# A new order of four queues in the middle of a one-core convolution and MLP kernel

## The chip, the cores and the metric

The kernel runs on one core of a Trainium2 chip. A core has five engines with an instruction queue each: TensorE (PE, matmuls, with PEld for its weight loads), VectorE (DVE), ScalarE (ACT), GpSimd (POOL) and SyncE (SP, which here only issues DMAs). Each queue runs in order; between queues there are semaphores. The metric is device time in microseconds (us) of one execution.

## The reference: what is computed

The inputs are x = A_q, k and v, each 2048 x 448 in bf16, filters for k, and the weights of an MLP that works along the 2048 positions. Cut to what matters:

```python
def _layernorm(x, axis=-1, eps=1e-5):
    ...
    return (x - m) / jnp.sqrt(v + eps)

    def _A_ref(q, k, v, shift_k, ssm_k, ssm_D):
        ...
        for t in range(ks):
            k_shift = k_shift + k_pad[:, t:t + S, :] * shift_k[:, ks - 1 - t][None, None, :]
        kv = k_shift * v
        ...
        y_f = kv_f * kf_f[None, :, :, :]
        ...
        y = y + kv * ssm_D[None, None, :]
        return q * y

    def _B_ref(x, w1, b1, w2, b2):
        h = _layernorm(x, axis=-1)
        u = jnp.einsum("bsd,sf->bdf", h, w1) + b1
        u = _gelu(u)
        y = jnp.einsum("bdf,fs->bds", u, w2) + b2
        ...

    x = A_q
    h = x + _A_ref(_layernorm(x, axis=-1), A_k, A_v, A_shift_k, A_ssm_k, A_ssm_D)
    h2 = h + _B_ref(_layernorm(h, axis=-1), B_w1, B_b1, B_w2, B_b2)
    return h2
```

kv_f and kf_f are the transforms of kv and of ssm_k, padded to twice the length: a causal convolution over 2048 positions.

## The kernel before

Positions are split as 128 partitions x 16 rows (position = 16 x partition + row). The convolution is a real transform made of matmuls in stages with a shuffle across partitions between them. In the order of the data:

- kv: transposes and small matmuls that apply the shift filter, multiplied by v (L1026).
- Stage 1 of the transform, "k1" for the filter and "u1" for kv (L1078): 16 steps each of 8 matmuls into a pair of PSUM banks. One evacuation copies the pair (128 x 896) to SBUF (op 8, L1088, or L1086 where ssm_D is added). Behind every second step three DMAs shuffle what two evacuations left (ops 9 and 10 on POOL, op 11 on SP, L1094): k1.3:9 is op 9 of step k1.3 and carries steps 2 and 3 of that block.
- Stage 2, "k2" and "u2" (L1113): 16 steps each of 4 matmuls into a pair of banks. Steps come in twos; the odd one carries the two evacuations (ops 4 and 5; L740 on ACT and L743 on DVE for k2, which scale; L739 and L742 for u2). An evacuation needs the matmuls of both steps, as it overwrites what they read.
- Products and the inverse's first stage, "i1": 16 products on DVE (L1180, 128 x 1792, op 0 of a step; a ring of four buffers), and eight groups of 16 matmuls (L1197) with two evacuations each (ops 9 and 18, or 8 and 17; L739, L742). Four DMAs behind a group shuffle its result (L1221; L1208 for the last group, i1.16). The first product waits for all shuffles of stage 1.
- The inverse's second stage "i2", one row after the other (L1323, L1329), with the gate q = layernorm(x): rows 0 to 3 are normalised beforehand ("xn", L1290 on ACT, L1292 on DVE); of the others the gate multiplies by 1/std first (L1339 on ACT, L1341 on DVE). Then a combination with x (L1349, L1359), and the statistics of the result: its sum from DVE, its squares from ACT (L1377), and a chain of five small instructions on POOL for two rows at a time (L1387, L1390, L1392, L1397 and L1401, a power of -1/2), behind which DVE writes the normalised row (L1408).
- The MLP: "mlp.r" for r = 0 to 15 are 7 matmuls of row r with the first half of w1 (L1455), accumulating over all rows into seven banks; mlp.17 to mlp.23 are those with the second half (L1465), gelu on ACT (L1445), then the second product (L1477) with the last addition on DVE (L1480).
- Beside it: "q" are the statistics of x, step q.(g+1) for rows 2g and 2g+1 (bn_stats L1257 as ops 0 and 2, aggregates L1259 as ops 1 and 3; ops 4 and 5 on POOL add epsilon, L1265, and take the power, L1268; for rows 4 to 15 they stand in every second step and serve four rows). "ct" are transposes of the table E into ET (L1127; ct0 the first eight, ct.0 to ct.2 the others), each group with one 16-bit copy of 128 x 1024 (L739 or L742). "ew" prepares a table on POOL, "warm" are two spare matmuls.

The order of the instructions isn't found by a compiler here. The program builds a list of operations, and the table ORDER gives each engine's queue word for word as step:op (a range where ops follow each other). An operation that two engines can do runs on the one whose table names it. A second table, SLOTS, names the PSUM bank (0 to 7) that each group of matmuls gets. Waits follow from that: an instruction waits for what it reads, and the first matmul of a group for the evacuation of the group that had its bank before.

```python
            self.eng[W].wait_ge(self.csem[E], n)
...
        FX = ("act", "dve")
...
                    for q_, a, nu in (("pool", 0, 8), ("pool", 96, 8), ("sp", 32, 16)):
...
                    aft = [x for w in wbufs for x in w.readers] if i == 0 else [mfirst[0]]
```

The first of these lines makes the waits of one engine for another, the second says which engines may evacuate, the third are the three shuffles behind stage 1, and the last is what the products wait for.

Of the kernel before, what the change touches and what calls it, by code (L numbers as in the profile page):

```python
# [30 lines left out]
        "mlp.19:4 mlp.7:0 mlp.19:5 mlp.8:0 mlp.19:6 mlp.7:4 mlp.9:0 mlp.9:2 mlp.8:6 mlp.9:6 mlp.8:1 mlp.9:5 mlp.9:1 "
        "mlp.8:4 mlp.10:2 mlp.10:1 mlp.10:6 mlp.9:4 mlp.19:7 mlp.10:0 mlp.10:5 mlp.10:4 mlp.10:3 mlp.11:0 mlp.11:5 "
        "mlp.11:3-4 mlp.11:1-2 mlp.11:6 mlp.12:0-6 mlp.13:0-6 mlp.14:6 mlp.14:4 mlp.14:1 mlp.14:5 mlp.14:3 mlp.15:6 "
        "mlp.15:5 mlp.15:4 mlp.15:1 mlp.19:8-15 mlp.14:0 mlp.21:0-15 mlp.17:0-8 mlp.14:2 mlp.20:0-7 mlp.22:0-7 "
        "mlp.17:9-15 mlp.20:8-15 mlp.18:0-15 mlp.15:2 mlp.23:0-7 mlp.15:0 mlp.22:8-15 mlp.15:3 mlp.23:8-15 "
        "mlp.24:0-13 mlp.25:0-13 mlp.26:0-13 mlp.27:0-13 mlp.28:0-13 mlp.29:0-13 mlp.30:0-13 mlp.31:0-13 mlp.32:0-13 "
        "mlp.33:0-13 mlp.34:0-13 mlp.35:0-13 mlp.36:0-13 mlp.37:0-13 mlp.38:0-13 mlp.39:0-10 mlp.39:16-17 mlp.39:11 "
        "mlp.39:18-20 mlp.39:12 mlp.39:21-22 mlp.39:13 mlp.39:23-29 "
# [4 lines left out]
        "k1.7:8 u1.6:8 tables.9:5 u1.8:8 u1.9:8 u1.10:8 k2.1:4-5 u1.12:8 u1.13:8 u1.14:8 u1.15:8 k2.9:5 k2.5:5 "  # L43
        "ct0.0:8 k2.7:4 k2.3:5 u2.1:4 k2.15:4-5 u2.13:4 u2.7:4-5 k2.11:4-5 u2.9:5 i1.1:9 i1.1:18 u2.11:5 i1.14:9 "
        "i1.14:18 u2.11:4 i1.10:18 i1.8:18 u2.5:5 u2.3:5 i1.10:9 u2.3:4 i1.12:18 i1.12:9 i1.6:18 u2.15:5 u2.15:4 "
        "i1.4:17 i1.4:8 i1.16:18 i1.16:9 xn.1:0 xn.5:0 xn.2:0 xn.4:0 ct.0:8 ct.1:8 ct.2:8 i2.46:0 i2.29:0 i2.19:0 "
        "i2.55:0 i2.22:0 i2.33:0 i2.59:0 i2.31:0 i2.35:0 i2.68:0 i2.72:0 i2.44:0 i2.48:0 i2.81:0 i2.57:0 i2.61:0 "
        "i2.94:0 i2.70:0 i2.98:0 i2.74:0 i2.83:0 i2.87:0 i2.96:0 i2.100:0 mlp.16:5-6 mlp.16:1 mlp.21:16 mlp.17:16 "
# [8 lines left out]
        "u1.7:8 k1.2:8 k1.3:8 q.1:1 q.3:0 q.1:2 q.2:0 k2.13:4 q.1:3 q.2:1 k2.13:5 u1.11:8 q.2:3 q.3:2 k2.9:4 k2.5:4 "  # L57
        "q.4:2 k2.7:5 k2.3:4 u2.1:5 i1.0:0 u2.13:5 i1.1:0 i1.14:0 i1.13:0 u2.9:4 i1.8:0 q.4:3 i1.7:0 i1.10:0 i1.9:0 "
        "i1.8:9 i1.12:0 u2.5:4 i1.11:0 i1.6:0 q.3:3 q.4:0 i1.5:0 i1.3:0 xn.0:1 q.4:1 i1.2:0 i1.6:9 i1.16:0 i1.15:0 "
        "q.3:1 q.5:2 q.6:2 q.5:3 xn.3:1 q.6:0 q.7:2 q.5:0-1 q.6:1 q.6:3 q.8:0 q.8:2 q.7:0 q.7:3 i2.3:0 i2.11:0 "  # L60
        "i2.4:0 i2.12:0 i2.5:0 i2.13:0 i2.6:0 i2.14:0 i2.18:0 i2.8:0 i2.21:0 i2.30:0 i2.16:0 q.8:1 i2.42:0 i2.34:0 "
        "bias.1:0 i2.26:0 q.8:3 i2.27:0 q.7:1 i2.47:0 i2.43:0 q.8:4 i2.56:0 i2.39:0 i2.60:0 i2.40:0 i2.85:0 i2.52:0 "
        "i2.53:0 i2.73:0 i2.69:0 i2.95:0 i2.65:0 i2.66:0 i2.82:0 i2.86:0 i2.99:0 i2.78:0 i2.79:0 i2.105:0 i2.92:0 "
        "i2.91:0 i2.104:0 mlp.24:14 mlp.25:14 mlp.26:14 mlp.27:14 mlp.28:14 mlp.29:14 mlp.30:14 mlp.31:14 mlp.32:14 "
        "mlp.33:14 mlp.34:14 mlp.35:14 mlp.36:14 mlp.37:14 mlp.38:14 mlp.39:14 mlp.39:30 "
# [8 lines left out]
        "tables.9:10 u1.9:9-10 k1.3:9-10 tables.9:9 u1.13:9-10 q.1:4 u1.11:9 u1.15:10 u1.15:9 u1.11:10 tables.9:11 "  # L74
        "q.1:5 ew.0:3 ew.0:0 q.2:4 xn.0:0 ew.0:1-2 i1.1:19 i1.1:21 i1.14:19 i1.14:21 i1.8:19 i1.8:21 i1.10:19 "
        "i1.10:21 i1.12:19 i1.12:21 q.2:5 i1.6:19 i1.6:21 i1.6:20 i1.4:20 i1.16:21 q.4:4 xn.3:0 i1.16:22 q.6:4-5 "
        "q.4:5 i1.4:19 i1.4:21 i2.7:0 i2.15:0 i2.23:0-2 i2.24:0 i2.25:0 i2.36:0-2 i2.37:0 i2.38:0 q.8:5 i2.49:0-2 "
        "i2.50:0 i2.51:0 i2.62:0-2 i2.63:0 i2.64:0 i2.75:0-2 i2.76:0 i2.88:0 i2.77:0 i2.88:1 i2.101:0-1 i2.88:2 "
        "i2.101:2 i2.102:0 i2.89:0 i2.90:0 i2.103:0 i2.0:0 "
# [30 lines left out]
        "mlp.39:16:1 "  # L110
# [1429 lines left out]
```

## Time and profile before

| what | us |
|---|---|
| runs (3), median | 171.01 |
| lowest and highest run | 170.82 and 174.45 |
| the profiled execution, its own time | 170.75 |
| span of the profiled execution, first to last instruction | 168.9 |
| busy in the span: PE, DVE, ACT, POOL | 160.1, 99.8, 92.5, 60.2 |

Some 1.85 us of the profiled execution's time lie outside its span. TensorE is busy 95% of the span by the records, but a matmul record lasts longer than the time to the next matmul, so this says little of single stages; the waits and the stretches say more. In a row of a timeline stand the start in us, the time up to the end of the last instruction in it, engine, line, operation, output<-input with shapes, the count, and in brackets the idle time just before and what ended it. In a row of the stretches each engine has its busy time, with the number of its instructions in brackets.

### The profile page before, as it was taken

Reading aid. Unit: us, or ns where it says so; the run is one execution under the profiler, and the core shown is the slowest. Engines: PE = TensorE matmul, PEld = TensorE weight load, DVE = VectorE, ACT = ScalarE, POOL = GpSimd, SP = SyncE. Lnnn points to the kernel's source line nnn. Section 1 sums busy time; section 2 is a strip of 40 time slices with the busy share of each in tenths; the row PEclk is TensorE's granted clock in tenths of the full one; section 3 lists DMA queues with packets and bytes.
Section 4 is the critical chain, followed back from the end, with each engine's and each line's share of the span. In section 5 each row is a group of like instructions: output and inputs, shape, how many; then the busy total and the mean of one; then the engine's idle time right before and its main releaser. Section 6 shows DMA issues by size and latency. Waiting matters only on the chain.

```text
span 168.9 us, 3572 instructions
## 1 busy us (share of the span) xinstructions
PE 160.1 (95%) x1416; PEld 92.8 (55%) x1416; DVE 99.8 (59%) x197; ACT 92.5 (55%) x134; POOL 60.2 (36%) x157
## 2 busy tenths in 40 slices
PE   6999999888998999889999999999999999999994
PEld 2885775423323433344445555555577777777783
DVE  4978898999999999999879230000003213132231
ACT  3699868899999999999787703103550000000000
POOL 8103749997910545885887800000000000000000
PEclk9999999999999999999999999999999999999999
DMA  5999799887749456658999999930000111101111
GB/s 162 420 331 385 243 307 347 307 319 241 231 99 352 128 187 183 194 165 276 390 400 402 426 419 420 415 131 0 0 0 7 51 54 54 54 0 58 54 54 54
DMA packets 15564, 35.15 MB, mean 208 GB/s; under 512 B 3804, under 2 KB 9644, under 8 KB 15548
## 3 DMA queue, kind: packets, MB, share of 16 engines
q1 hardware_dynamic: 12396, 28.26, 45.8%
q0 software_dynamic: 3008, 6.58, 12.1%
q8 instruction: 11, 0.18, 0.4%
q10 hardware_dynamic: 144, 0.08, 0.2%
q14 instruction: 5, 0.04, 0.1%
HBM read 22.05 MB, written 1.84 MB: 141 GB/s over the span
## 4 chain that ended last, share of the span: by engine, by line
PE 67%; DVE 13%; ACT 8%; POOL 6%; issue 2%; DMA 2%; DVEq 0%; ACTq 0%; POOLq 0%
PE ps L1477 25%; PE ps L1465 13%; PE ps L1455 11%; DVE arena L1180 6%; ACT arena L740 4%; POOL arena L1094 4%; PE ps L985 3%; PE ps L1044 3%; PE ps L1057 3%; ACT arena L739 3%; PE ps L1078 2%; PE ps L1197 2%; ACT arena L1088 2%; DMA arena<-arena 2%; DVE arena L742 2%
## 5 line engine op out<-in xcount | busy, mean ns | idle before, releaser
L1480 DVE SCALAR_TENSOR_TENSOR arena<-ps,arena 128x448 bf16<-128x448 f32 (+2 forms) x17 | 11.1, 656 | 57.0 <-PE ps L1477 57.0
L1477 PE MATMUL ps<-arena 128*128 128x448 bf16 (+2 forms) x238 | 42.7, 342 | 0.0
L1477 PEld LDWEIGHTS ps<-arena 128*128 128x128 bf16 x238 | 33.3, 145 | 9.5
L1455 PE MATMUL ps<-arena 128*128 128x448 bf16 x112 | 24.8, 353 | 0.2
L1465 PE MATMUL ps<-arena 128*128 128x448 bf16 x112 | 23.3, 352 | 0.0
L739 ACT CAST arena<-ps 128x896 bf16<-128x896 f32 x26 | 21.8, 968 | 0.6 <-PE ps L1113 0.2
L1088 ACT CAST arena<-ps 128x896 bf16<-128x896 f32 x24 | 20.3, 914 | 2.1 <-PE ps L1078 1.6
L1445 ACT ACTIVATE arena<-ps,arena 128x448 bf16<-128x448 f32 x14 | 8.2, 632 | 20.4 <-PE ps L1465 10.3
L1094 POOL DMA_DIRECT2D arena<-arena x32 | 17.9, 562 | 3.5 <-ACT arena L1088 2.9
L1180 DVE TENSOR_TENSOR arena<-arena 128x1792 bf16<-128x1792 bf16 x16 | 16.8, 1083 | 0.1
L1455 PEld LDWEIGHTS ps<-arena 128*128 128x128 bf16 x112 | 10.8, 98 | 11.0 <-DVE arena L1408 1.5
L1113 PE MATMUL ps<-arena 128*64 128x448 bf16 x128 | 15.7, 361 | 1.0 <-ACT arena L739 0.5
L1465 PEld LDWEIGHTS ps<-arena 128*128 128x128 bf16 x112 | 11.0, 98 | 10.2
L1078 PE MATMUL ps<-arena 128*32 128x448 bf16 x256 | 14.8, 355 | 1.6 <-DVE arena L1026 0.5
L1197 PE MATMUL ps<-arena 64*128 64x448 bf16 x128 | 13.7, 351 | 1.1 <-DVE arena L1180 0.5
L1221 POOL DMA_DIRECT2D arena<-arena x16 | 9.5, 596 | 14.0 <-ACT arena L739 13.5
L1113 PEld LDWEIGHTS ps<-arena 128*64 128x64 f16 x128 | 5.2, 108 | 10.8 <-ACT arena L739 3.2
L1197 PEld LDWEIGHTS ps<-arena 64*128 64x128 f16 x128 | 5.1, 94 | 9.5 <-ACT arena L739 3.4
L739 ACT COPY arena<-ps 128x1024 bf16<-128x1024 bf16 (+2 forms) x10 | 9.4, 966 | 1.7 <-PE ps L985 1.5
L1026 DVE TENSOR_TENSOR arena<-ps,arena 128x512 bf16<-128x512 f32 (+1 forms) x16 | 9.4, 619 | 0.7 <-PE ps L1011 0.7
L1078 PEld LDWEIGHTS ps<-arena 128*32 128x32 f16 x256 | 5.2, 95 | 8.3 <-ACT arena L1088 1.7
L1408 DVE TENSOR_SCALAR arena<-arena 128x448 bf16<-128x448 f32 x16 | 7.7, 511 | 3.5 <-POOL arena L1401 3.5
(102 smaller groups left out, 198.3 us busy)
## 6 DMA issues: line engine op xcount, KB each, us to landing
arena<-in_B_w_dram SPq DMA_DIRECT2D x8, 896.0 KB, 10.0
arena<-in_B_w_dram SPq DMA_DIRECT2D x2, 2048.0 KB, 17.4
arena<-arena SPq DMA_DIRECT2D x16, 224.0 KB, 3.6
arena<-arena POOLq DMA_DIRECT2D x32, 112.0 KB, 3.3
arena<-in_B_w_dram SPq DMA_DIRECT2D x2, 1536.0 KB, 19.3
arena<-arena POOLq DMA_DIRECT2D x13, 196.0 KB, 3.8
arena<-in_A_k_dram SPq DMA_DIRECT2D x4, 448.0 KB, 5.5
arena<-in_A_v_dram SPq DMA_DIRECT2D x4, 448.0 KB, 8.4
```

The source lines that it names most:

```text
L739: return e.copy(out=dst(), in_=src())
L1078: op("pe", lambda e, W, b=b, r=r, q=q, x=x, c0=c0: e.matmul(PS[32 * q:32 * q + 32, b.slots[x], 0:D], E[:, 2 * r + x, c0:c0 + 32], src[:, r ...
L1088: return e.copy(out=dst, in_=Ppair(b)) if W == "act" else e.tensor_copy(out=dst, in_=Ppair(b))
L1094: shuf[tag].append(op(q_, lambda e, W, g=g, i=i, a=a, nu=nu, jh=jh: e.dma_start(T[a + i:a + i + 4 * nu - 3:4].rearrange("p (j k) c d -> p ...
L1113: op("pe", lambda e, W, b=bs[h], h=h, j=j, c=c, par=par: e.matmul(PS[64 * par:64 * par + 64, b.slots[c], 0:D], FW[:, 64 * c:64 * c + 64], ...
L1180: op("dve", lambda e, W, m=m, i=i: e.tensor_tensor(out=MR(m.slots[0]).rearrange("p (x y) d -> p x y d", x=2), in0=TU[:, i].unsqueeze(2).br ...
L1197: k = op("pe", lambda e, W, b=bs[h], m=ms[h], par=par, t=t, tab=tab, xy=xy, P=P: e.matmul(Pb(b, par), tab[P, :], MR(m.slots[0])[P, xy, :], ...
L1221: op(q_, lambda e, W, j=j, p0=p0, a=a, b_=b_, j0=j0: e.dma_start(TZ[p0:p0 + 29:4, j0:j0 + (b_ - a) // 8].rearrange("p r c d -> p r (c d)") ...
L1455: op("pe", lambda e, W, r=r, fc=fc, b=bs[fc]: e.matmul(Pb(b), W1A[:, r, 128 * fc:128 * fc + 128], Q[:, r, :], start=(r == 0), stop=(r == R ...
L1465: op("pe", lambda e, W, r=r, fc=fc, b=b: e.matmul(Pb(b), W1B[:, r, 128 * (fc - n0):128 * (fc - n0) + 128], Q[:, r, :], start=(r == 0), sto ...
L1477: op("pe", lambda e, W, r=r, fc=fc, b=b, d0=d0, d1=d1: e.matmul(Pb(b)[:, d0:d1], W2[fc // 7][:, fc % 7, r:S:R], G[:, fc, d0:d1], start=(fc ...
L1480: op("dve", lambda e, W, r=r, b=b, A=A, d0=d0, d1=d1: e.scalar_tensor_tensor(out=XR(r)[:, d0:d1], in0=Pb(b)[:, d0:d1], scalar=bm[:, r:r + ...
```

## The change

Only the two tables change. The PE, ACT, DVE and POOL rows are in another order from behind the evacuation of k1.3 (DVE), behind u1.9's first shuffle (POOL), behind k2.1 (ACT) and behind k2.0 (PE) up to the end of i2. Twelve operations go from ACT to DVE (ct0.0:8, k2.15:5, k2.3:5, k2.5:5, u1.14:8, u2.1:4, u2.3:5, u2.7:4, u2.9:5, xn.1:0 and the gates i2.59:0 and i2.81:0), eleven from DVE to ACT (k2.13:5, k2.3:4, k2.5:4, u1.11:8, u2.1:5, u2.13:5, u2.9:4, i1.6:9, i1.8:9 and the gates i2.42:0 and i2.85:0). SP's order and the number of instructions are as before, and POOL's DMAs keep their order among themselves. PSUM banks are given out anew from ct0 on. Of the diff, the head of DVE's changed part:

```diff
-        "u1.7:8 k1.2:8 k1.3:8 q.1:1 q.3:0 q.1:2 q.2:0 k2.13:4 q.1:3 q.2:1 k2.13:5 u1.11:8 q.2:3 q.3:2 k2.9:4 k2.5:4 "
+        "u1.7:8 k1.2:8 k1.3:8 q.1:1 q.2:3 q.1:2 q.3:0 q.4:2 q.1:3 q.2:0 q.3:1 q.2:1 q.4:3 ct0.0:8 k2.13:4 q.3:2 "
```

What stands in the queues, as queue rows (number, line, operation, output<-input, count, and for POOL the semaphores it waits for). First POOL from the shuffles of u1.9 and k1.3 to those of u1.11, before:

```order
68 L1094 DMA arena<-arena 8x4x1792 [waits csem_act]
69 L1094 DMA arena<-arena 8x4x1792
70 L1094 DMA arena<-arena 8x4x1792 [waits csem_dve]
71 L1094 DMA arena<-arena 8x4x1792
72 L891 TENSOR_TENSOR arena<-arena 128x128
73 L1094 DMA arena<-arena 8x4x1792 [waits csem_act]
74 L1094 DMA arena<-arena 8x4x1792
75 L1265 TENSOR_SCALAR arena<-arena 128x2 [waits csem_dve]
76 L1094 DMA arena<-arena 8x4x1792 [waits csem_dve]
77 L1094 DMA arena<-arena 8x4x1792 [waits csem_act]
78 L1094 DMA arena<-arena 8x4x1792 x2
```

And now:

```order
68 L1094 DMA arena<-arena 8x4x1792 [waits csem_act]
69 L891 TENSOR_TENSOR arena<-arena 128x128
70 L894 TENSOR_SCALAR arena<-arena 128x128 [waits csem_pool]
71 L1265 TENSOR_SCALAR arena<-arena 128x2 [waits csem_dve]
72 L1094 DMA arena<-arena 8x4x1792 x3
73 L1094 DMA arena<-arena 8x4x1792 [waits csem_act]
74 L1094 DMA arena<-arena 8x4x1792
75 L1094 DMA arena<-arena 8x4x1792 [waits csem_act]
76 L1265 TENSOR_SCALAR arena<-arena 128x2
77 L1094 DMA arena<-arena 8x4x1792 [waits csem_dve,csem_act]
78 L1094 DMA arena<-arena 8x4x1792 x2
```

The statistic q.1:4 (L1265) has moved from behind u1.13's two DMAs to a place between u1.9's first and second; rows 72 are u1.9:10 and both of k1.3. A second one, q.2:4, now stands ahead of u1.15's and u1.11's last DMAs.

DVE in the same place, from the statistics behind k1.3 to the first product (L1180), before:

```order
59 L1088 CAST arena<-ps 128x896
60 L1259 BN_AGGR arena<-arena 128x2
61 L1257 BN_STATS arena<-arena 128x6
62 L743 TENSOR_SCALAR arena<-ps 128x896 x2
63 L1257 BN_STATS arena<-arena 128x6
64 L743 TENSOR_SCALAR arena<-ps 128x896 x2
65 L742 CAST arena<-ps 128x896
66 L1180 TENSOR_TENSOR arena<-arena 128x1792
67 L742 CAST arena<-ps 128x896
68 L1180 TENSOR_TENSOR arena<-arena 128x1792 x3
```

And now:

```order
57 L1257 BN_STATS arena<-arena 128x6
58 L1259 BN_AGGR arena<-arena 128x2 x3
59 L742 COPY arena<-ps 128x1024
60 L743 TENSOR_SCALAR arena<-ps 128x896
61 L1257 BN_STATS arena<-arena 128x6
62 L743 TENSOR_SCALAR arena<-ps 128x896 x2
63 L1088 CAST arena<-ps 128x896
64 L743 TENSOR_SCALAR arena<-ps 128x896 x3
65 L742 CAST arena<-ps 128x896 x2
66 L1180 TENSOR_TENSOR arena<-arena 128x1792 x2
67 L742 CAST arena<-ps 128x896
68 L1180 TENSOR_TENSOR arena<-arena 128x1792 x7
```

The copy of ct0 (L742 COPY) has come to DVE, nine evacuations instead of eight lie ahead of the first product, and behind the second product there is one evacuation and then seven products in a row.

Last POOL's chain of the i2 statistics, from the power of rows 2 and 3 to that of rows 6 and 7, before:

```order
87 L1401 TENSOR_TENSOR arena<-arena 128x2
88 L1387 TENSOR_SCALAR arena<-arena 128x2
89 L1390 TENSOR_TENSOR arena<-arena 128x2
90 L1392 TENSOR_TENSOR arena<-arena 128x2
91 L1397 TENSOR_SCALAR arena<-arena 128x2
92 L1401 TENSOR_TENSOR arena<-arena 128x2
93 L1268 TENSOR_TENSOR arena<-arena 128x4
94 L1387 TENSOR_SCALAR arena<-arena 128x2
```

And now:

```order
86 L1401 TENSOR_TENSOR arena<-arena 128x2
87 L1221 DMA arena<-arena 8x2x896
88 L1387 TENSOR_SCALAR arena<-arena 128x2
89 L1390 TENSOR_TENSOR arena<-arena 128x2
90 L1268 TENSOR_TENSOR arena<-arena 128x4
91 L1392 TENSOR_TENSOR arena<-arena 128x2
92 L1387 TENSOR_SCALAR arena<-arena 128x2
93 L1397 TENSOR_SCALAR arena<-arena 128x2
94 L1401 TENSOR_TENSOR arena<-arena 128x2
```

A DMA of i1.4 (L1221), which stood ahead of the chain, and the power q.8:5 (L1268) now lie inside it, and sums of the next two rows (the second L1387) go ahead of a power.

106 rows, old and new, of tables (ORDER, SLOTS) are left out of this document.

## The prediction

> **What bounds the kernel now.** I read the table of stretches first, then the groups of instructions by line, the waits, and last the timelines of single engines.
>
> ```profile
> core 0: us, PE busy (x) PEld busy (x) DVE busy (x) ACT busy (x) POOL busy (x), PEclk, DMA share, GB/s
> 36.00:55.00 19.00, 17.14 (x172) 6.00 (x168) 18.97 (x27) 18.69 (x24) 9.62 (x21) 1.00 0.71 234
> 55.00:71.00 16.00, 14.83 (x141) 5.63 (x137) 15.87 (x25) 15.65 (x20) 9.64 (x16) 1.00 0.59 173
> 71.00:76.00 5.00, 4.10 (x32) 2.36 (x33) 4.78 (x13) 5.00 (x8) 4.39 (x9) 1.00 0.57 170
> 82.20:124.00 41.80, 41.80 (x222) 21.46 (x223) 12.69 (x36) 18.28 (x39) 12.24 (x30) 1.00 0.72 285
> ```
>
> From 82.2 us on TensorE has no idle time at all, and the matmuls there are the same in number before and after the change. Before that, from 36 to 71 us, it is ScalarE (18.69 of 19.00 and 15.65 of 16.00) and VectorE (18.97 and 15.87) that are full: they drain PSUM, and TensorE waits for free banks. So the change is worth what it moves the moment at which the dense matmuls begin, and nothing else. The waits say the same:
>
> ```profile
> PEld ps L1197 <- ACT arena L739: 3.4, 10, 0.6
> PEld ps L1113 <- ACT arena L739: 3.2, 7, 0.7
> PEld ps L1197 <- DVE arena L1180: 1.5, 2, 1.0
> ```
>
> The prices of one instruction come from the groups (busy time, mean ns):
>
> ```profile
> L739 ACT CAST arena<-ps 128x896 bf16<-128x896 f32 x26 | 21.8, 968 | 0.6 <-PE ps L1113 0.2 <-PE ps L1197 0.2
> L742 DVE CAST arena<-ps 128x896 bf16<-128x896 f32 x6 | 6.5, 1085 | 0.0
> L742 DVE COPY arena<-ps 128x1024 bf16<-128x1024 bf16 x9 | 5.8, 685 | 1.1 <-PE ps L1057 1.1
> L1257 DVE BATCH_NORM_STATS2 arena<-arena 128x6 f32<-128x448 bf16 x16 | 9.2, 612 | 0.0
> ```
>
> Instructions of one engine overlap a little at their ends, so what counts is start to start. On the timelines:
>
> ```profile
> 36.30 1.73 ACT L740 ACTIVATE arena<-ps 128x896 bf16<-128x896 f32 x2
> 42.86 1.01 ACT L739 COPY arena<-ps 128x1024 f16<-128x1024 f16 x1
> 43.75 1.80 ACT L740 ACTIVATE arena<-ps 128x896 bf16<-128x896 f32 x2
> 45.77 0.91 ACT L739 CAST arena<-ps 128x896 bf16<-128x896 f32 x1 [0.22 <-PE ps L1113]
> 52.37 12.40 ACT L739 CAST arena<-ps 128x896 bf16<-128x896 f32 x15
> 67.39 3.69 ACT L739 CAST arena<-ps 128x896 bf16<-128x896 f32 x4
> 33.98 2.09 DVE L1086 TENSOR_TENSOR arena<-ps,arena 128x896 bf16<-128x896 f32 x2
> 36.20 1.68 DVE L1257 BATCH_NORM_STATS2 arena<-arena 128x6 f32<-128x448 bf16 x3
> 47.03 1.08 DVE L1180 TENSOR_TENSOR arena<-arena 128x1792 bf16<-128x1792 bf16 x1
> 69.06 0.18 DVE L1259 BATCH_NORM_AGGREGATE arena<-arena 128x2 f32<-128x6 f32 x1
> 59.88 0.57 PE L1113 MATMUL ps<-arena 128*64 128x448 bf16 x4 [0.24 <-ACT arena L739]
> 60.47 0.93 PE L1197 MATMUL ps<-arena 64*128 64x448 bf16 x8
> ```
>
> With a backlog ScalarE takes an evacuation every (12.40-0.97)/14 = 0.82 us. The 1024-wide copy ct0 costs it 43.75-42.86 = 0.89. VectorE's evacuations and products follow each other at 1.085-0.085 = 1.00, its 16-bit copies at 0.60, statistics at 0.53 (three took 1.68). A group of four matmuls takes 0.57, one of eight 0.93, each about 0.1 behind the drain that frees its bank. ScalarE's last drain of this stage ends at 67.39+3.69 = 71.08; VectorE's last product ends at about 69.1, where the aggregate stands.
>
> **The change, part by part.** Counting the tables: 12 instructions go from ScalarE to VectorE (ct0, eight evacuations, xn.1, two gates i2.59 and i2.81), 11 go back (nine evacuations, gates i2.42 and i2.85). SyncE's order is unchanged.
>
> Work up to the last product: ScalarE loses eight evacuations and ct0 and gains nine, 0.82-0.89 = -0.07 us. VectorE loses nine, gains eight and ct0, 0.60-1.00 = -0.40. No row has an f16 copy on VectorE; between the bf16 copy of that size (0.60) and the f32 pace stretched to 1024 (1.00 x 1024/896 = 1.14) I take the row with 16-bit data. The page "VectorE: DVE Perf Modes" of the Trainium skill (Why PSUM operands drop a tier) lets any 16-bit PSUM copy run up to twice as fast as an f32 one; that too would be 0.60 here, where the f32 pace would leave -0.40+0.54 = +0.14. The six statistics ahead of the last product stay six, in other places: nothing.
>
> So the sums give at most a few tenths; the waits decide. I walk the new order with the spacings above, each matmul group starting 0.1 behind the drain of its banks. ScalarE: k2.1 twice from 36.30, u1.12, k2.13, u1.13, k2.5, k2.9, u1.11, u1.15, k2.15, k2.3, k2.7: the twelfth ends at 46.9, where before the twelfth ended at 45.77+0.91 = 46.68, with waits of 0.1 to 0.2 for matmuls on five of them. VectorE: the first product i1.0 starts at 48.97 instead of 47.03, with one evacuation and the copy (1.6) more behind it, so 0.3 of waits. Then u2.7 waits for its matmuls, which wait for banks that ScalarE drains (u2.13): about 0.45 idle between i1.1 and u2.7. From there VectorE has 18 more products and evacuations, one statistic and small ones: the last product ends at 69.2, against 69.1. ScalarE runs on at 0.82 and less, waits about 0.3 at i1.6, and drains i1.16 by 71.2 against 71.08. VectorE's gain of 0.40 is eaten by its two new waits. Term: +0.1.
>
> Shuffles: on POOL a statistic (q.1:4) now stands ahead of three DMAs (u1.9, and both of k1.3). It needs the aggregate of row 1, which VectorE reaches behind k1.3, two aggregates and three statistics.
>
> ```profile
> 36.18 2.18 POOL L1094 DMA_DIRECT2D arena<-arena  x4
> 39.92 1.12 POOL L1094 DMA_DIRECT2D arena<-arena  x2 [1.09 <-ACT arena L1088]
> DMA to landing us min/median/max: 3.9/4.0/4.4
> DMA to landing us min/median/max: 2.8/2.8/2.9
> DMA to landing us min/median/max: 3.3/3.4/3.7
> ```
>
> (The landing lines are those of POOL's L1094 issued from 36 to 38.5, from 39 to 41.2 and from 41.2 to 44.) Before, the four of 36.18 (u1.9, k1.3) went out without a break and the last began at 37.8. Now: k1.3's evacuation ends at 36.07, statistics run to 37.9, aggregate to 38.05, q.1:4 to 38.35, then three issues of 0.55, so k1.3's last begins at 39.45, 1.65 later. Behind it stand u1.13's issues, which wait for ScalarE until 40.4 anyway. Who needs k1.3: the groups k2.14 and k2.15, which by the walk could start at 42.95. With 3.4 to landing it is there at 42.85: no wait. With 2.8 the same; with 4.4 it lands at 43.85 and TensorE, then ScalarE and VectorE, stand 0.9. In the same way u1.11's last DMA starts at 45.1 (behind q.2:4), landing at 48.5 (up to 49.5), against the first product at 48.97: 0, up to 0.5. I take +0.1 for both together, since the middle row hides them and its margins are 0.1 and 0.5; ends 0 and +1.4. The page "DMA: Bandwidth & Descriptors" of the Trainium skill (Anatomy of one DMA) gives 2.0 us + bytes/436e3 for such a transfer; its estimate for 112 KB is 2.26 us, k1.3 landing at 41.7 and this term at 0. The trace disagrees: none of these rows is under 2.8.
>
> From the last drain to the dense matmuls:
>
> ```profile
> 71.13 1.69 PE L1323 MATMUL ps<-arena 128*128 128x448 bf16 x8 [0.26 <-ACT arena L739]
> 75.55 2.82 PE L1329 MATMUL ps<-arena 128*128 128x448 bf16 x14 [0.76 <-DMA arena<-arena]
> 78.77 0.59 POOL L1387 TENSOR_SCALAR arena<-arena 128x2 f32<-128x2 f32 x1 [0.66 <-DVE arena L1359]
> 80.47 1.07 POOL L1401 TENSOR_TENSOR arena<-arena 128x2 f32<-128x2 f32 x1
> 81.58 0.52 DVE L1408 TENSOR_SCALAR arena<-arena 128x448 bf16<-128x448 f32 x1 [0.52 <-POOL arena L1401]
> 82.14 0.68 PEld L1455 LDWEIGHTS ps<-arena 128*128 128x128 bf16 x5 [0.57 <-DVE arena L1408]
> 96.92 6.43 PE ps L1455 x34
> ```
>
> The transposes ct.1, ct.2, ct.0 now all run ahead of i2.9 and i2.1, while ScalarE still drains i1.16: cover instead of idle, but the matmuls i2.45 wait for the last transfer of i1.16 (row at 75.55), and that is issued behind ScalarE's last drain, so they start 0.1 later and the transposes gain nothing. Then i2.54, moved to fourth, waits about 0.3 for the bank of i2.45 (gate i2.46), and VectorE's statistics, 0.6 longer in front of i2.3 with xn.1 among them, make the first two normalised rows 0.6 to 1.0 late. None of it reaches the end: the third row's matmuls (mlp.2) are 32 matmuls behind i2.45 in both orders, 32 x 0.189 (6.43/34) = 6.06, and at 82.14 they waited for the chain from i2.21 over POOL (78.77, 80.47) to i2.26 (81.58). In the walk i2.21 starts at 78.03, before it started at 77.99; so this gate again moves 0.1, the same 0.1 as above.
>
> The tail of that chain:
>
> ```profile
> 95.58 1.38 POOL L1401 TENSOR_TENSOR arena<-arena 128x2 f32<-128x2 f32 x2
> 97.00 1.78 DVE L1408 TENSOR_SCALAR arena<-arena 128x448 bf16<-128x448 f32 x4 [2.18 <-POOL arena L1401]
> ```
>
> mlp.12 stands 120 matmuls behind i2.45 in both orders, at 98.83; its row came out of VectorE third of the last four, at 98.36. POOL now carries a DMA (i1.4:21, about 0.56) and i2.0 (0.2) inside this chain instead of outside, and the pow of rows 8 and 9 stands behind sums of rows 10 and 11. By the count of matmuls in front of them, rows 4, 5, 6, 8 and 9 of the MLP start 0.2 to 2.7 us later in the new order and rows 7, 10 and 11 up to 1.5 earlier; in the walk each of their rows is out of VectorE at least 0.3 before that, so only mlp.12 is tight: POOL ends its last pow between 97.0 (nothing lost) and 97.75, and mlp.12 waits 0 to 0.7. I take 0.2.
>
> Sum against the profiled execution (170.75 us; span 168.9): 170.75 + 0.1 + 0.1 + 0.2 = 171.15, forecast 171.2. The median of the runs shown, 171.01, lies 0.26 above that execution and one of the three lies 3.4 above it.
>
> **The rivals.** Faster: ScalarE's order may really close its waits. From 36.30 to 71.08 it took 34.78 us for 41 drains; at 0.82 throughout it would need 33.6, so up to 1.1 us goes, and the time is 169.65 to 170.6. For it: eight evacuations that come in pairs are now split over both engines (k2.13, k2.5, k2.9, k2.15, k2.3, u2.9, u2.1), so one pair's banks come free together. Against: VectorE is as full, and my walk gives the waits back. Slower, by one mechanism: k1.3's last shuffle lands later than 3.5 us from its issue. From there on each tenth is a tenth on both draining engines; at 4.4 it is +0.9, and 171.15-0.1+0.9 = 171.95, with u1.11's at its end 172.5. For it: the nearest window (36 to 38.5) has 3.9 to 4.4. Against: the issues are now spread out as in the window with 2.8. A third, that POOL's tail sets the end, is 171.65 at its end of +0.7, and lies in the forecast's own range.
>
> **How the numbers follow.** Forecast (170.6 to 171.8): 0.52. Faster order (down to 169.65): 0.25. Late shuffle (171.8 to 172.6): 0.15. Something not seen: 0.08. The range 169.5 to 172.7 takes both rivals in. A difference of 2%, 3.4 us, is about what a measurement of this kernel can tell from no change; no bound above reaches it, so faster and slower than that get only what is unseen: 0.03 and 0.04, within 2% 0.93.
>
> **What would show it.** Right: ScalarE's last i1 drain at 71.2 within 0.3; VectorE's first product near 49.0; q.1:4 ahead of k1.3's DMAs with their last issue near 39.5; i2.45 near 75.65; mlp.2 near 82.2; no gap on TensorE behind 82.3 but at mlp.12. Wrong: a gap of over 0.3 on TensorE before k2.14 (late shuffle), or the last i1 drain before 70.5 (faster order), or more than 0.5 us idle on TensorE behind 83 us (a chain I took as covered).

## The result, and the profile after

| | before | changed |
|---|---|---|
| median of the runs, us | 171.58 | 173.52 |
| a second series, us | 171.20 | 173.46 |
| profiled execution: own time, us | 170.75 | 173.75 |
| its span, us | 168.9 | 171.9 |

The changed kernel is slower: ratio 1.0124, 95% interval 1.0092 to 1.0155, and in the second series 1.0129 (1.0101 to 1.0158). That is about 2.1 us: less than the 2% that the prediction named as the least difference to count, but clear of noise here, as neither interval comes near 1, and 0.8 us above the range's upper end.

The profiled execution of the changed kernel is 3.0 us longer than that of before, and this splits in two. One half comes from its first 13 us, code that is the same in both kernels (TensorE's timeline with three waits that before doesn't have, and the start of k2.1; the last column in brackets is the idle time ahead and what ended it):

```profile
7.75 0.96 PE L1057 MATMUL ps<-arena 128*128 128x128 bf16 x12 [0.20 <-DMA arena<-in_A_ssm_k_dram]
9.01 0.71 PE L1057 MATMUL ps<-arena 128*128 128x128 bf16 x8 [0.30 <-DMA arena<-in_A_ssm_k_dram]
12.72 0.49 PE L1057 MATMUL ps<-arena 64*128 64x64 bf16 x5 [0.30 <-DMA arena<-in_A_ssm_k_dram]
36.80 0.95 PE L1113 MATMUL ps<-arena 128*64 128x448 bf16 x8
```

TensorE waits for loads of the filter, and k2.1 (L1113, the first matmuls of stage 2, still the same in both orders) starts at 36.80 where it started at 35.31 before. In twelve profiles of this study (the first one of each hybrid below is left out: one took 577 us, the other had half the clock from 14.4 to 17.8 us) k2.1 starts between 35.13 and 36.80, with the same instructions ahead of it; the changed kernel profiled again starts it at 35.87, the one before again at 35.13, and one with the front of before (the late shuffle in the order before, below) at 36.03. So these 1.49 us are chance. The other half, 1.51 us, lies between the start of k2.1 and the end, and from here on stages are compared by their distance from the start of k2.1.

The stretches of the changed kernel, each 1.49 to 1.55 later than those shown of before:

```profile
37.49:56.49 19.00, 17.48 (x174) 6.27 (x172) 18.86 (x28) 18.66 (x23) 10.17 (x21) 1.00 0.67 215
56.49:72.49 16.00, 15.08 (x147) 6.14 (x144) 15.87 (x25) 15.76 (x21) 9.85 (x17) 1.00 0.63 197
72.49:77.49 5.00, 3.73 (x27) 1.82 (x25) 4.93 (x14) 4.75 (x7) 3.07 (x7) 1.00 0.54 154
83.75:125.55 41.80, 40.78 (x215) 20.54 (x214) 12.49 (x35) 17.42 (x38) 13.81 (x32) 1.00 0.72 286
```

The drain stage (first two rows) is as full as before. The last row is the difference: before, TensorE was busy 41.80 of 41.80 with 222 matmuls, now 40.78 with 215. So time is lost behind the point where the matmuls should be dense. TensorE's timeline there:

```profile
84.64 0.54 PE L1329 MATMUL ps<-arena 128*128 128x448 bf16 x2
85.02 1.11 PE L1455 MATMUL ps<-arena 128*128 128x448 bf16 x5
86.84 0.55 PE L1329 MATMUL ps<-arena 128*128 128x448 bf16 x2 [0.71 <-DVE arena L1341]
87.23 1.11 PE L1455 MATMUL ps<-arena 128*128 128x448 bf16 x5
88.25 0.54 PE L1329 MATMUL ps<-arena 128*128 128x448 bf16 x2
95.91 0.36 PE L1455 MATMUL ps<-arena 128*128 128x448 bf16 x1 [0.31 <-DVE arena L1408]
```

The rows at 84.64, 86.84 and 88.25 are i2.80, i2.84 and i2.93 (rows 12, 13 and 14 of the sequence); the one at 95.91 is mlp.8:2. In a dense stretch a matmul record begins 0.16 before the one ahead of it ends, so a wait costs its bracket and 0.16: 0.87 at i2.84, 0.47 at mlp.8. Who is late shows on VectorE and POOL:

```profile
86.10 0.68 DVE L1341 TENSOR_SCALAR arena<-ps,arena 128x448 f32<-128x448 f32 x1 [0.94 <-POOL arena L1268]
95.34 0.93 DVE L1408 TENSOR_SCALAR arena<-arena 128x448 bf16<-128x448 f32 x2 [0.61 <-POOL arena L1401]
```

```profile
81.85 1.05 POOL L1401 TENSOR_TENSOR arena<-arena 128x2 f32<-128x2 f32 x1
82.86 0.69 POOL L1221 DMA_DIRECT2D arena<-arena  x1
83.63 0.36 POOL L1387 TENSOR_SCALAR arena<-arena 128x2 f32<-128x2 f32 x1
84.08 0.52 POOL L1390 TENSOR_TENSOR arena<-arena 128x2 f32<-128x2 f32 x1
84.56 1.50 POOL L1268 TENSOR_TENSOR arena<-arena 128x4 f32<-128x4 f32 x1
...
93.00 0.59 POOL L1387 TENSOR_SCALAR arena<-arena 128x2 f32<-128x2 f32 x1 [1.24 <-DVE arena L1349]
93.67 0.50 POOL L1390 TENSOR_TENSOR arena<-arena 128x2 f32<-128x2 f32 x1
94.13 1.17 POOL L1401 TENSOR_TENSOR arena<-arena 128x2 f32<-128x2 f32 x1
```

Read upwards from i2.84: its bank comes free with the gate i2.81 (L1341), the gate multiplies by 1/std of row 12, and that is the power q.8:5 (L1268), which ends at 86.06. On POOL the shuffle i1.4:21 (L1221) and two sums (i2.36:0-1) now stand ahead of it. Later the power i2.64 (94.13) stands behind the sums i2.75, for which POOL waited 1.24 us with its inputs for i2.64 long there.

The second profile of the changed kernel shows one thing more, at the same places of TensorE's timeline:

```profile
85.87 0.55 PE L1329 MATMUL ps<-arena 128*128 128x448 bf16 x2 [0.73 <-DVE arena L1341]
86.26 1.11 PE L1455 MATMUL ps<-arena 128*128 128x448 bf16 x5
88.39 0.55 PE L1329 MATMUL ps<-arena 128*128 128x448 bf16 x2 [1.02 <-DMA arena<-arena]
```

Here i2.93 waits 1.18 for a transfer, and mlp.8 for nothing. The transfer is i1.4:21 itself: by the code it is one of those that carry the last two rows of the sequence,

```python
                    for g_, a, b_, j0 in (("zpool", 0, 112, 0), ("zsp", 112, 128, 14)):
```

and i2.93 is row 14. (i1.4:19 is the other one on POOL.) The query of L1221's issues behind 81 us gives its time to landing, in the second profile:

```profile
DMA to landing us min/median/max: 6.5/6.5/6.5
```

and in the first:

```profile
DMA to landing us min/median/max: 5.3/5.3/5.3
```

Issued at 81.88 it lands at 88.38, and i2.93 starts at 88.39. In the first profile it landed at 82.86 + 5.3 = 88.16, when i2.93 was held up by i2.84 anyway. Before, it was issued at 75.34.

### The profile page after: what moved, and what is told of

It reads as the page before. It is cut to its first block, busy times and chain, and to the rows that moved or that the text cites. A ratio compares the mean times of both kernels' runs of the same rounds, so it can differ in the third digit from the quotient of the medians.

```text
span 171.9 us, 3571 instructions
## 1 busy us (share of the span) xinstructions
PE 161.3 (94%) x1416; PEld 93.1 (54%) x1416; DVE 100.2 (58%) x198; ACT 92.5 (54%) x133; POOL 61.9 (36%) x157
## 4 chain that ended last, share of the span: by engine, by line
PE 57%; DVE 12%; ACT 10%; DMA 8%; POOL 5%; issue 4%; SPq 2%; DVEq 0%; POOLq 0%
PE ps L1477 24%; PE ps L1465 12%; ACT arena L739 8%; PE ps L1455 6%; DMA arena<-in_A_ssm_k_dram 6%; PE ps L1078 5%; PE ps L1011 3%; PE ps L1113 3%; POOL arena L1401 3%; DMA arena<-arena 2%; DVE arena L1180 2%; DVE arena L1257 2%; DVE arena L743 2%; PE ps L985 1%; DVE arena L1026 1%
## 5 line engine op out<-in xcount | busy, mean ns | idle before, releaser
L1455 PE MATMUL ps<-arena 128*128 128x448 bf16 x112 | 24.5, 353 | 0.4 <-DVE arena L1408 0.3
L1465 PE MATMUL ps<-arena 128*128 128x448 bf16 x112 | 23.5, 352 | 0.0
L739 ACT CAST arena<-ps 128x896 bf16<-128x896 f32 x27 | 22.5, 988 | 0.5 <-PE ps L1197 0.2
L1088 ACT CAST arena<-ps 128x896 bf16<-128x896 f32 x24 | 20.5, 914 | 2.1 <-PE ps L1078 1.6
L1180 DVE TENSOR_TENSOR arena<-arena 128x1792 bf16<-128x1792 bf16 x16 | 16.6, 1082 | 0.1
L1113 PE MATMUL ps<-arena 128*64 128x448 bf16 x128 | 15.7, 360 | 0.8 <-ACT arena L740 0.2
L1221 POOL DMA_DIRECT2D arena<-arena x16 | 9.6, 603 | 11.9 <-ACT arena L739 11.9
L1113 PEld LDWEIGHTS ps<-arena 128*64 128x64 f16 x128 | 5.6, 108 | 10.6 <-ACT arena L739 3.3
L739 ACT COPY arena<-ps 128x1024 bf16<-128x1024 bf16 (+2 forms) x9 | 8.6, 964 | 3.2 <-PE ps L1057 1.6
L1329 PE MATMUL ps<-arena 128*128 128x448 bf16 x32 | 7.6, 353 | 2.0 <-DMA arena<-arena 1.0
```

Source lines behind the costliest of these rows:

```text
L739: return e.copy(out=dst(), in_=src())
L1088: return e.copy(out=dst, in_=Ppair(b)) if W == "act" else e.tensor_copy(out=dst, in_=Ppair(b))
L1113: op("pe", lambda e, W, b=bs[h], h=h, j=j, c=c, par=par: e.matmul(PS[64 * par:64 * par + 64, b.slots[c], 0:D], FW[:, 64 * c:64 * c + 64], ...
L1180: op("dve", lambda e, W, m=m, i=i: e.tensor_tensor(out=MR(m.slots[0]).rearrange("p (x y) d -> p x y d", x=2), in0=TU[:, i].unsqueeze(2).br ...
L1455: op("pe", lambda e, W, r=r, fc=fc, b=bs[fc]: e.matmul(Pb(b), W1A[:, r, 128 * fc:128 * fc + 128], Q[:, r, :], start=(r == 0), stop=(r == R ...
L1465: op("pe", lambda e, W, r=r, fc=fc, b=b: e.matmul(Pb(b), W1B[:, r, 128 * (fc - n0):128 * (fc - n0) + 128], Q[:, r, :], start=(r == 0), sto ...
```

## The experiments

The theories. W (after the first profile): the drain stage is neutral, and the waits at i2.84 and mlp.8 are the loss; W1 is W with nothing else, W2 adds the late landing of i1.4:21 at i2.93. D: the new order of drains and shuffles costs it. G: the gates cost it, because they changed engine. All edits are in the two tables. The measured column "to end" is from the start of k2.1 to the end of the last matmul, and the waits are start-to-start excess on TensorE's timeline (bracket + 0.16). The kernel before against itself is at 1.0028, so a difference of 0.003 between two ratios says nothing.

| kernel | ratio to before (95%) | to end, us | i2.84 | i2.93 | mlp.8 |
|---|---|---|---|---|---|
| before; again | 1; 1.0028 (0.9995-1.0060) | 131.16; 131.31 | 0 | 0 | 0 |
| changed | 1.0124 (1.0092-1.0155) | 132.67 | 0.87 | 0.08 | 0.47 |
| changed, again | 1.0129 (1.0101-1.0158) | 133.22 | 0.89 | 1.18 | 0 |
| new front, old back | 0.9992 (0.9962-1.0023), 0.9992 (0.9966-1.0018) | 131.60 | 0 | 0 | 0 |
| old front, new back | 1.0108 (1.0066-1.0151) | 133.35 | 0.93 | 1.42 | 0 |
| shuffle early | 1.0039 (1.0009-1.0070) | 131.87 | 0.24 | 0.08 | 0.48 |
| shuffle early, power late | 1.0043 (1.0014-1.0072) | 131.95 | 1.07 | 0.08 | 0 |
| power ahead of shuffle | 1.0200 (1.0165-1.0234) | 135.24 | 0 | 2.43 | 0 |
| gates swapped back | 1.0111 (1.0083-1.0139) | 133.53 | 1.09 | 1.11 | 0 |
| i2.64 early only | 1.0141 (1.0106-1.0176) | 133.12 | 0.87 | 1.38 | 0 |
| three moves | 1.0002 (0.9973-1.0031) | 131.26 | 0 | 0.08 | 0 |
| before, shuffle late | 1.0075 (1.0047-1.0103) | 132.56 | 0.04 | 0.04 | 0 |

In the two profiles of the change the waits add up to the loss behind i2.45 (the i2 matmuls that wait for i1's last transfer). The first took 132.67 - 40.34 = 92.33 from there to the end, where before took 131.16 - 40.24 = 90.92: 1.41 more, against waits of 0.87 + 0.08 + 0.47. The second took 2.0 more, against 0.89 + 1.18.

**Front or back?** Two hybrids, cut behind the last i1 evacuation. Each operation that stands on the other side of the cut in the other order was put at the head of the back part, or kept where the front has it; the banks of the back part were renamed to fit (0, 1 for 6, 7).

```diff
-front (to i1.16:9) and back (ct, i2, mlp) of the changed order
+front of the changed order, back of the order before
+front of the order before, back of the changed order
```

> Everything up to the last i1 group in the changed order, everything behind it (tables, i2, MLP) in the order before. Theory W (the loss is two waits in i2: the matmuls i2.84 for the gate i2.81, which waits for the power q.8:5 on POOL, about 0.87 us, and mlp.8 for the power i2.64 behind the sums i2.75, about 0.47 us; the drain stage gives and takes nothing; the 1.44 us by which the first transposes waited longer for their loads in the changed kernel's profile are chance): time as before within 0.4 us, ratio 0.998 to 1.003, i2.84 and mlp.8 without a wait. Rival D (the new order of drains and shuffles costs it, by way of memory traffic or of waits that the one profile hides): ratio 1.008 to 1.015, as the changed kernel.

> The reverse: up to the last i1 group the order before, behind it the changed order. Theory W: slower than before by 1.2 to 1.6 us, ratio 1.007 to 1.010, with both waits in its trace (0.7 to 0.9 at i2.84, 0.3 to 0.5 at mlp.8). Rival D: as before, ratio 0.998 to 1.003.

The new front costs nothing (0.9992), the new back alone costs what the change costs (1.0108, just above the 1.010 that W gave). D falls. In the profile of the new back the granted clock is 1.00 from 17.8 us on, and behind the old front it has the waits at i2.84 (0.93) and, where W named none, at i2.93:

```profile
91.01 0.55 PE L1328 MATMUL ps<-arena 128*128 128x448 bf16 x2 [1.26 <-DMA arena<-arena]
```

A second run of the first hybrid was made for its trace:

> The front of the changed order with the back of the order before, once more, for a trace. Theory W2: 131.2 us from k2.1 to the end of the last matmul, within 0.3, as before; last i1 drain 35.8 behind the start of k2.1, i2.45 40.2 behind it; no wait at i2.84, i2.93 or mlp.8. Rival D: over 131.8 us with the excess ahead of i2.45.

None of the three waits is there, and the ratio is 0.9992 again. The 131.60 miss the expectation by 0.1: i2.45 started 40.47 behind k2.1, where it depends on a transfer; in the profiles of this study it lies between 39.96 and 40.98, whichever the order, so single profiles can't place such a part of a microsecond.

**The shuffle alone.** POOL's queue:

```diff
-i1.4:19 i2.7:0 i2.15:0 i2.23:0-2 i2.24:0 i2.25:0 i1.4:21 i2.36:0-1 q.8:5 i2.36:2
+i1.4:19 i1.4:21 i2.7:0 i2.15:0 i2.23:0-2 i2.24:0 i2.25:0 i2.36:0-1 q.8:5 i2.36:2
```

> The changed kernel with one shuffle's issue on POOL (i1.4:21, 0.64 us) put back ahead of i2.7, where POOL has 0.67 us idle, instead of into the chain ahead of q.8:5. Theory W: q.8:5 ends 0.6 us earlier, the gate i2.81 with it, the wait at i2.84 shrinks from 0.87 to 0.2 to 0.3, and the time by 0.5 to 0.65 us against the changed kernel (ratio to before about 1.009). Rival G (the gate is late because it changed engine, and stands in VectorE's queue): no change.

The wait at i2.84 shrank as expected (0.24), which speaks against G. But the ratio fell to 1.0039, some 1.45 us (0.0085 x 171) faster than the changed kernel instead of 0.6. So theory W lacked a part, and that is how the landing at i2.93 was found. What is left is mostly mlp.8 (lines in this kernel have numbers lower by one):

```profile
93.51 0.36 PE L1454 MATMUL ps<-arena 128*128 128x448 bf16 x1 [0.32 <-DVE arena L1407]
```

The next two tell the issue of the shuffle from the power.

**Power first, and power late.** POOL's queue; in the first also VectorE's q.7:1 and q.8:4 moved up behind q.8:3:

```diff
-i2.25:0 i1.4:21 i2.36:0-1 q.8:5 i2.36:2
+i2.25:0 q.8:5 i1.4:21 i2.36:0-2
```

> The changed kernel with q.8:5 moved ahead of the shuffle i1.4:21 and of the sums i2.36 on POOL (q.7:1 and q.8:4 moved up on VectorE). The gate i2.81 is then early and i2.84 waits for nothing, but the shuffle is issued 1.1 to 1.5 us later, near 84. Theory W2 (the late issue of i1.4:21 is a third wait: rows 14 and 15, from i2.93 on, need its landing, 4 to 6.8 us behind the issue): the wait moves to i2.93, 0.5 to 2 us, ratio 1.008 to 1.018, no faster than the changed kernel. Rival W1 (the gate alone costs it): i2.84 and i2.93 without a wait, the fourth row's normalised product up to 0.6 late, ratio 1.005 to 1.010, at least 0.3 us faster than the changed kernel.

```diff
-i1.4:19 i2.7:0 ... i2.25:0 i1.4:21 i2.36:0-1 q.8:5 i2.36:2
+i1.4:19 i1.4:21 i2.7:0 ... i2.25:0 i2.36:0-2 q.8:5
```

> The changed kernel with i1.4:21 ahead of i2.7 as in the run of the early shuffle, and q.8:5 moved back behind i2.36's third sum, so that it ends about as late as in the changed kernel. Theory W2: the wait at i2.84 is there (0.6 to 0.9 us), none at i2.93; ratio 1.006 to 1.010, some 0.3 to 0.6 us faster than the changed kernel. Rival W1: as the changed kernel, 1.010 to 1.015.

TensorE's waits between 80 and 92 us, first with the power ahead of the shuffle, then with the shuffle early and the power late:

```profile
88.53 0.83 PE L1329 MATMUL ps<-arena 128*128 128x448 bf16 x2 [2.27 <-DMA arena<-arena]
```

```profile
85.01 0.55 PE L1329 MATMUL ps<-arena 128*128 128x448 bf16 x2 [0.91 <-DVE arena L1341]
```

With the gate early and the shuffle later still, i2.84 is free and i2.93 waits 2.43 (2 was the most expected): the slowest kernel of the study, and W1, by which nothing waits at i2.93, falls. But its ratio of 1.0200 lies above W2's 1.018, and its profile took 95.00 from i2.45 to the end, 4.08 more than before. The wait is 2.43 of that. The rest, 1.65, is TensorE's clock, by the stretches of this profile (third column from the right):

```profile
88.50:92.30 3.80, 3.77 (x11) 1.57 (x12) 2.19 (x7) 1.28 (x3) 1.18 (x4) 0.55 1.04 403
92.30:96.00 3.70, 3.70 (x21) 1.95 (x20) 3.03 (x10) 3.36 (x10) 3.14 (x6) 1.00 1.05 418
```

Right behind the wait the granted clock is 0.55, and 11 matmuls take the 3.8 us in which 20 would fit at 0.19 each. Four of this kernel's six runs have a mean clock of 0.99; the two at 1.00 took 173.69 and 174.17, which is 1.015 and 1.017 of the 171.20 of before, inside W2's range. So about 0.004 of the 1.0200 comes with the lower clock and not from the wait alone.

With the shuffle early and the gate as late as ever, i2.93 is free and the ratio is 1.0043, lower than the 1.006 that W2 gave as its least. The table shows why a longer wait at i2.84 costs so little there: i2.84 waits 0.83 more than with the early shuffle alone, but then mlp.8's 0.48 is gone, because its matmuls come later and i2.64 is done by then. The 0.35 that remain don't show in the ends (131.87 and 131.95), as i2.45 started 0.22 earlier in the second, and are too small for the ratios.

**The engine of the gates.** i2.81 back on ScalarE, i2.85 back on VectorE:

```diff
-act: i2.48:0 i2.85:0 i2.57:0        dve: i2.47:0 i2.81:0 i2.56:0 i2.39:0
+act: i2.48:0 i2.81:0 i2.57:0        dve: i2.47:0 i2.56:0 i2.85:0 i2.39:0
```

> The changed kernel with the gates i2.81 and i2.85 on the engines they had before (i2.81 on ScalarE, i2.85 on VectorE behind i2.56); everything else as changed. Theory W: i2.81 waits for q.8:5 there too, i2.84 still waits 0.6 to 0.9 us, ratio 1.009 to 1.015. Rival G (the change of engine makes the gate late): no wait at i2.84, 0.8 us faster than the changed kernel, ratio 1.004 to 1.008.

```profile
85.88 0.55 PE L1329 MATMUL ps<-arena 128*128 128x448 bf16 x2 [0.93 <-ACT arena L1339]
88.33 0.55 PE L1329 MATMUL ps<-arena 128*128 128x448 bf16 x2 [0.95 <-DMA arena<-arena]
```

The same two waits, the first now ended by ScalarE instead of VectorE (1.09, a little above the expected 0.9), ratio 1.0111. G falls: which engine runs the gate doesn't matter, since q.8:5 is late for both.

**The last power alone.**

```diff
-i2.63:0 i2.75:0-1 i2.64:0 i2.75:2
+i2.63:0 i2.64:0 i2.75:0-2
```

> The changed kernel with i2.64 ahead of the sums i2.75 on POOL, and nothing else. Theory W2: mlp.8's wait of 0.47 showed only in the one execution in which i1.4:21 landed early (5.3 us); where it lands after 6.5 us, i2.93's wait covers it. So little changes: ratio 1.009 to 1.014, and no wait at mlp.8 in the trace. Rival W1 (the three waits add up): 0.47 us faster than the changed kernel, ratio 1.009 to 1.011, which is within the first range; the trace of waits decides between them.

```profile
85.32 0.55 PE L1329 MATMUL ps<-arena 128*128 128x448 bf16 x2 [0.71 <-DVE arena L1341]
88.04 0.55 PE L1329 MATMUL ps<-arena 128*128 128x448 bf16 x2 [1.22 <-DMA arena<-arena]
```

No gain (1.0141, expected up to 1.014): with the shuffle late, i2.93's wait covers mlp.8's.

**All three.** i1.4:21 ahead of i2.7, q.8:5 ahead of i2.36 with q.7:1 and q.8:4 moved up, i2.64 ahead of i2.75:

> The changed kernel with three moves: i1.4:21 ahead of i2.7 as in the run before; q.8:5 ahead of the sums i2.36 on POOL, with q.7:1 and q.8:4 moved up on VectorE; i2.64 ahead of the sums i2.75. The gates stay on their new engines. Theory W: no wait at i2.84 or at mlp.8, 1.2 to 1.4 us faster than the changed kernel, ratio to before 1.001 to 1.005. Rival G (the gates' change of engine costs it): the wait at i2.84 stays, at most 0.5 us faster. Rival D: as the changed kernel, ratio about 1.012.

TensorE's only waits between 76 and 125 us (line numbers again lower by one):

```profile
76.09 3.44 PE L1328 MATMUL ps<-arena 128*128 128x448 bf16 x16 [0.35 <-DMA arena<-arena]
79.75 1.12 PE L1454 MATMUL ps<-arena 128*128 128x448 bf16 x5 [0.22 <-DVE arena L1407]
```

Ratio 1.0002 (0.9973 to 1.0031), 131.26 to the end: five operations moved on two queues undo the loss, with the gates, the order of TensorE and the whole front as the change has them. W expected at least 1.001, as it did not have the landing at i2.93, which the early shuffle undoes too.

**The late shuffle in the order before.** POOL's queue of before:

```diff
-i1.4:19 i1.4:21 i2.7:0 i2.15:0 i2.23:0-2 i2.24:0 i2.25:0 i2.36:0-2
+i1.4:19 i2.7:0 i2.15:0 i2.23:0-2 i2.24:0 i2.25:0 i1.4:21 i2.36:0-2
```

> The kernel before with one move: the shuffle i1.4:21 on POOL from ahead of i2.7 to behind the power i2.25, where the changed kernel has it. Everything else as before. Theory W2: issued near 81.6, it lands 5.3 to 6.6 us later, 86.9 to 88.2; i2.93 stands 1.9 us later behind i2.45 in this order (12.1 instead of 10.2) and waits 0 to 0.5. In POOL's chain it puts i2.38 0.6 later, and the fourth row's matmuls, which had 0.17 of slack behind i2.39, wait 0.3 to 0.5. Together ratio 1.002 to 1.006. Rival (the late shuffle costs its landing in any order): 1.2 us at i2.93, ratio 1.007 to 1.010. Rival (harmless alone): 0.998 to 1.002.

```profile
82.74 0.68 POOL L1221 DMA_DIRECT2D arena<-arena  x1
```

```profile
DMA to landing us min/median/max: 6.7/6.7/6.7
```

```profile
87.22 1.31 PE L1455 MATMUL ps<-arena 128*128 128x448 bf16 x6 [0.65 <-DVE arena L1408]
```

It lands at 89.4 and i2.93, at 89.79 in this order, doesn't wait; the wait is at the fourth row's matmuls (87.22), behind POOL's chain. So far as W2 said, but it is 0.8 instead of 0.3 to 0.5, and the ratio 1.0075 is above W2's range. The rival that gave such a ratio put the loss at i2.93, where there is none. Of the 1.40 that this profile is longer than that of before, 0.66 lie behind i2.45; the other 0.74 are i2.45 itself, which started 40.98 behind k2.1, the latest of all. Whether the move makes it late isn't settled.

**Before, again.**

> The kernel before, once more, for the part before k2.1. If the loads of the first 12 us differ by chance, k2.1 starts between 35.2 and 37 here too, and from there to the end of the last matmul it takes 131.2 within 0.2. If 35.3 belongs to the order before, it is 35.3 again.

k2.1 started at 35.13 and the rest took 131.31; the loads were early in both profiles of before, so this run alone doesn't tell chance from order. The others do: with the front of before and the late shuffle k2.1 started at 36.03, with the changed front and the early shuffle at 35.19. And the change again:

> The changed kernel as it is, once more, for the size of the effect and for the part before k2.1. Theory W (waits in i2): from the start of k2.1 to the end of the last matmul 132.7 us, as in its first profile, against 131.2 before, more where i2.93 waits for the landing of i1.4:21; ratio 1.009 to 1.015. Chance in the loads: k2.1 starts anywhere from 35.2 to 37 us. If the late transposes belonged to the change, k2.1 would start at 36.8 again.

k2.1 at 35.87, 133.22 to the end, both waits as quoted.

No kernel here beats the one before by more than its interval.

## Why the prediction was wrong

By its own steps, in times from the start of k2.1 (35.31 before, 36.80 in the first profile after):

- **Drain stage, +0.1.** Right. The last matmul of i1 starts 34.47 behind k2.1 in both profiles, and ScalarE's last drain ends at 35.77 before (71.08 - 35.31) and 35.76 after (72.56 - 36.80). The first product was put 13.66 behind k2.1 (48.97 - 35.31) and came at 13.63 (50.43 - 36.80). The rival by which ScalarE closes its waits didn't happen. The f16 copy ct0, now on VectorE, was priced at 0.60 from the bf16 rows and takes 0.57 to the start of the next instruction (40.64 - 40.07, VectorE's timeline after), as those rows had it:

```profile
40.07 0.66 DVE L742 COPY arena<-ps 128x1024 f16<-128x1024 f16 x1
40.64 1.08 DVE L743 TENSOR_SCALAR arena<-ps 128x896 bf16<-128x896 f32 x1
```

  By the Trainium skill's page "VectorE: DVE Perf Modes" (Why PSUM operands drop a tier) a VectorE operation with an operand in PSUM runs at up to twice the plain pace with 16-bit data and at the plain pace with f32. The trace agrees: 0.57 is half of the 1.14 that the f32 pace would give.

- **Shuffles k1.3 and u1.11, +0.1.** Right in kind: k2.14 waited for no transfer, and the hybrid with the new front is at 0.9992. The term was 0.
- **i2.45 and mlp.2, together the same +0.1.** Right: 40.34 against 40.24, and 46.90 against 46.84.
- **POOL's tail at mlp.12, +0.2.** Wrong place: mlp.12 waited for nothing.
- **"In the walk each of their rows is out of VectorE at least 0.3 before that, so only mlp.12 is tight".** This is the step that failed, and with it "None of it reaches the end" and the first premise, that the change is worth what it moves the moment at which the dense matmuls begin, "and nothing else": they began 0.1 later, as forecast, and then had to wait among themselves. The step followed the normalised rows, that is one of the two inputs of TensorE's stretch, and left out the i2 matmuls between them. These stand earlier in the new order: i2.84 comes 9.70 behind i2.45 (50.04 - 40.34, its wait of 0.87 included), before 10.78. Their conditions were not walked: a bank that the gate i2.81 frees, the gate's power q.8:5 on POOL, and the rows 14 and 15 that i1.4:21 carries. In place of no wait the two profiles of the change have 1.42 (0.87, 0.08 and 0.47) and 2.07 (0.89 and 1.18).
- **"POOL now carries a DMA (i1.4:21, about 0.56)".** The move was seen, and priced at what its issue costs POOL. Its landing was not priced: the issue comes 6 us later (46.06 instead of 40.03 behind k2.1), and the transfer then takes 5.3 to 6.5 instead of 1.9 to 2.9. That landing is the larger part: the early shuffle takes the ratio from 1.0124 to 1.0039, and still to 1.0043 where the power is late. There the transfer takes no less (6.7 and 6.3 us), but from an issue nearly 5 us earlier it is in time: what costs is the later issue, together with the earlier place of i2.93 (in the order before the late shuffle makes no wait there). The two other moves together take it to 1.0002; that last step is about as large as the noise.
- **The slower rival** had the right mechanism, a shuffle that lands late because POOL does other things first, at the wrong shuffle (k1.3). The prediction's sign for itself, "more than 0.5 us idle on TensorE behind 83 us (a chain I took as covered)", is what came.
- **The chances.** Within 2% was right at 0.93, but 2% is not "about what a measurement of this kernel can tell": the intervals here are about 0.3% to either side. The range ended at 172.7 because every bound in it came from terms that had been walked, and the 0.08 for what was not seen added nothing to its width.

The Trainium skill's page "DMA: Bandwidth & Descriptors" (Anatomy of one DMA), weighed in the prediction against the k1.3 shuffle, gives 2.0 us + bytes/436e3, an estimate of 2.07 us for the 28 KB of i1.4:21. Where the shuffle is issued ahead of the weight loads the traces agree within 0.3 us but for one (1.8, 1.9 and 1.8 us, once 2.9, for i1.4:19 and i1.4:21 in the two profiles of before); behind them they don't (4.7 to 6.7).

## What to carry to other kernels

When an issue of a DMA moves on a queue, price its landing at the new place and find the first reader in the new order; the half microsecond of the issue is the small part. When a matmul moves up among others, walk every condition of it anew (its data, its bank, and whatever frees the bank), also where its neighbours are what the change is about. And don't take a wait in a trace for what its removal is worth: the waits of one trace add up, but each ends when its own condition is met, so where an early one goes, a later one can appear or grow (0.08 to 2.43 at i2.93), and undoing one alone may show nothing.

## What the runs showed of the hardware

A 28 KB shuffle (i1.4:19 or i1.4:21) took 1.8 to 2.9 us from issue to landing when POOL issued it before the weight loads that SyncE starts at 75 to 77 us (L1428), and 4.7 to 6.7 us when it was issued behind the first of them, even by 0.3 us. This holds in all twelve profiles. But no run moved the loads, so that they are the cause is likely and not shown. From the kernel before again, the shuffles i1.4:19 and i1.4:21 (POOL's issues of L1221; duration of the issue, then first and last start):

```profile
L1221 POOL DMA_DIRECT2D arena<-arena x2: 557/580/602, 74.5 to 75.1; - x2
DMA to landing us min/median/max: 1.8/1.8/1.9
```

and SyncE's timeline with the first of these weight loads:

```profile
75.77 1.91 SPq L1428 DMA_DIRECT2D arena<-in_B_w_dram  x3
```

From the hybrid with the new front, run again, the same two views; the second shuffle went out at 76.0:

```profile
75.72 1.47 SPq L1428 DMA_DIRECT2D arena<-in_B_w_dram  x3
```

```profile
L1221 POOL DMA_DIRECT2D arena<-arena x1: 567/567/567, 76.0 to 76.0; - x1
DMA to landing us min/median/max: 5.0/5.0/5.0
```

In the changed kernel's second profile the stretches show how full the DMA engines get behind that point (last two columns, share and GB/s):

```profile
76.00:80.00 4.00, 3.70 (x18) 1.53 (x19) 3.83 (x14) 3.41 (x8) 2.81 (x6) 1.00 0.66 198
80.00:84.00 4.00, 4.00 (x23) 2.05 (x21) 4.00 (x13) 3.77 (x10) 3.42 (x7) 1.00 1.05 393
84.00:88.00 4.00, 2.64 (x14) 0.99 (x11) 2.45 (x8) 2.62 (x8) 3.67 (x8) 1.00 1.05 390
```

The shuffle doesn't stand behind all of the loads, by the table of issues of that profile (size, median us to landing):

```profile
arena<-in_B_w_dram SPq DMA_DIRECT2D x8, 896.0 KB, 10.2
arena<-in_B_w_dram SPq DMA_DIRECT2D x2, 2048.0 KB, 17.3
```

The same page of the Trainium skill (Queues, rings and completion order) has the DMA engines take turns between queues packet by packet, which would agree; no run here tests it.

POOL's power of 128 x 4 values (q.8:5) took 1.40 to 1.50 us in each kernel where it stands right behind the second sum of i2.36, and 1.00 to 1.15 in each where it stands elsewhere, on the same data. What stretches it stays open.

TensorE's granted clock fell to half once in the twelve profiles before the last matmul: with the power ahead of the shuffle, for 3.4 us (88.67 to 92.08) behind an idle time of 2.27 us. Behind the shorter idle times in the dense stretch of the other kernels, up to 1.22 us, it stayed at 1.00. That the wait brings it about is not shown.
